# Routing of two neighbouring 1024-token units in one set of instructions, in an agent-attention and top-1 mixture-of-experts kernel

## The chip, the cores and the metric

The kernel runs on one core of a Trainium2 chip. The metric is the device time of one launch in microseconds (us), taken as the median of several executions. A lower time is better.

## The reference

Four batches of 11456 tokens with 128 channels go through an attention with 49 agents, and then every token goes through one of eight experts.

```python
def sm(a, b):                                  # softmax of scaled products
    s = scale * (a @ b.transpose(0, 2, 1))
    e = np.exp(s - s.max(-1, keepdims=True))
    return e / (e.sum(-1, keepdims=True) + 1e-09)
agent_v = sm(agents, k) @ v                    # (4, 49, 128)
x = (sm(q, agents) @ agent_v).reshape(-1, 128) # 45824 tokens

logits = x @ w_gate                            # 8 experts
e_idx = np.argmax(logits, axis=1)
probs = softmax(logits)
gate_w = probs[np.arange(N), e_idx]
eom = 1.0 / (1.0 + np.exp(-(x @ w_output_gate)))
for e in range(E):
    mask = e_idx == e
    h = np.maximum(x[mask] @ w1[e], 0.0)       # 128 -> 1024
    out[mask] = gate_w[mask, None] * eom[mask, e, None] * (h @ w2[e])
```

## The kernel before

**Tiling.** A batch is cut into twelve units (`UNITS`, line 21): eleven of 1024 tokens (128 partitions by 8 tokens) and a last one of 192 tokens (96 partitions by 2). For each batch the kernel makes the agents' averages from k and v, then guesses the expert that most tokens of the batch will take (`fold`, line 666), and runs all tokens of the batch through that one expert in a dense main stream (`mm1` and `mm2`, lines 1009 and 1041, two tiles of 512 tokens for each unit). Tokens that choose another expert are counted, and are computed again afterwards in 14 small "leftover" tiles (`left_prepare`, `left_static`, from line 1377), fetched by indirect DMAs and written over the first result.

**The main stream.** For each tile, TensorE makes hidden values `h` into PSUM banks 0 to 3; ScalarE writes their half-precision upper part `hh` (a relu), VectorE the remainder `hl` (line 1037); then TensorE multiplies both with the second weight into `y`. ScalarE and VectorE add the two halves of `y` into `os` (`finish`, line 1061), GpSimd multiplies `os` by the factor `smt` of each token, and SyncE stores it (`store`, line 1078). `store` begins only when the factor of the unit is in the dictionary `SM`.

**The q side of a unit** (`q_rest`, line 845) has these steps. TensorE has put the scores `qs` into a bank. VectorE takes the maximum `qm` and the difference `qz` (lines 853 to 855), and the bank is free. ScalarE takes the exponential `ef`; ScalarE and GpSimd make a half-precision pair `e16`; SyncE issues a transposing DMA into `x1` and four copies into `x2`. TensorE multiplies `x1` by the gates into `lg` (line 887). ScalarE copies one half of that (`lL`), VectorE adds the other half and makes `d256`. Here `rests[me]` becomes 2. What follows, lines 903 to 933, is called the routing here: 14 VectorE instructions (`rr` twice, `ll`, `lm`, `ld_`, `lr`, `rm`, `oh`, `og`, `ogs`, `se`, `a_` twice, `lT`) and two ScalarE exponentials (`lex`, `eo`), each over the 8 tokens of a partition; then GpSimd makes `smt`, puts the factor beside `ef` and writes the tokens that leave the guessed expert into the table `oht` (lines 936 to 941). SyncE stores `ef` to DRAM (`efd`), and `rests[me]` becomes 3.

**What sets the order.** No instruction order is written by hand. Each part is a Python generator that yields what it would issue next; a planner (`Clock`, line 50) holds an estimated time for each engine and tile from fixed costs (`Engine.cost`, line 153) and lets a generator go on when its inputs should be ready. The result is one fixed instruction list for each engine, which the chip runs in order. `small_products` (line 990) walks through the k, q and v units in a fixed list; `roomy` (line 838) keeps a q unit at most some four units ahead of the main stream, and asks that the logits of the unit five before it are there (`rests` over 1). `q_rest` itself begins only when the unit three before it is wholly done:

```python
while me > 2 and rests[me - 3] < 3 or me > 1 and not state.get(0, {}).get("w"):
    yield None
```

While it waits there it holds the bank of its scores, and `wait_free(True)` allows two such banks at a time. Banks 4 to 7 serve everything but `h`.

In the third batch's end `left_index` (line 1218) begins to put gathers of the leftover tiles into the stream, with VectorE instructions (on tile `big`, shown as `bigs`) that wait for what they bring.

Of the kernel before, what the change touches and what calls it, by code (L numbers as in the profile page):

```python
# [7 lines left out]
F32 = mybir.dt.float32  # L8
# [4 lines left out]
ALU = mybir.AluOpType  # L13
# [3 lines left out]
P = 128  # L17
B, N, C, A, E, F = 4, 11456, 128, 49, 8, 1024
A2 = 50
NB = F // P  # L20
UNITS = [(u * 1024, 128, 8) for u in range(11)] + [(11264, 96, 2)]
# [7 lines left out]
PHASES = [(0, 3, 13, 384), (3, 1, 1, 128)]  # L29
# [213 lines left out]
def agent_attention_top1_moe(ctx, tc, qT, kT, v, aT, wg, wo, w1, w2, cst, out):  # L243
    nc = tc.nc
    clk = Clock()
    ACT, DVE, POOL = Engine(clk, "ACT", nc.scalar), Engine(clk, "DVE", nc.vector), Engine(clk, "POOL", nc.gpsimd)
    PE, SY = Engine(clk, "PE", nc.tensor), Engine(clk, "SP", nc.sync)

    def pool(name, bufs):
        return Tiles(clk, ctx.enter_context(tc.tile_pool(name=name, bufs=bufs)), bufs)  # L250
# [3 lines left out]
    wk = pool("wk", 2)  # L254
# [34 lines left out]
    def release(k):  # L289
        banks[k][0] = True  # L290
# [34 lines left out]
    rank8 = kc[:, K_RANK:K_RANK + E]  # L325
# [17 lines left out]
    for i in range(4):  # L343
        t = cp.tile([P, 8, P], F16, name=f"e16_{i}")
        e16s.append(t)
    avd = []
    for i in range(2):
        t = cp.tile([P, 2, P], F32, name=f"avd_{i}")
# [3 lines left out]
    for i in range(2):  # L352
        t = cp.tile([P, 2, 18], F16, name=f"gs_{i}")
# [3 lines left out]
    for i in range(2):  # L357
        t = cp.tile([P, E, NCOL], F32, name=f"oht_{i}")
# [9 lines left out]
    efd = [dr.tile([n * N, A2], F32, name=f"efd{b0}") for b0, n, _, _ in PHASES]  # L368
# [49 lines left out]
    state = {}  # L418
    picking = [True]
    X1 = {}  # L420
    SM = {}
# [56 lines left out]
    def vacant_turned():  # L478

        return first_place(LARGE, LARGE + SMALL) or first_place(0, LARGE, KEEP)  # L480

    def place(item, k, shape, dt=F32):
        kind, b, u = item
        t = ld.tile([P] + shape, dt, name=f"{kind}{b}_{u}_ld", tag=f"ld{k}", bufs=1)
        places[k] = [False, t.name]
        held[item] = k
        return t
# [51 lines left out]
    NU = len(UNITS)  # L539
# [295 lines left out]

    rests = []

    def roomy(me, n):

        if me < n:  # L840
            return True
        b, u = tiles[max(mains[0] - 1, 0)][0:2]
        return NU * b + u > me - n and rests[me - n] > 1

    def q_rest(b, u, s, mark):
        base, pp, nt = UNITS[u]
        me = len(rests)
        rests.append(0)
        while me > 2 and rests[me - 3] < 3 or me > 1 and not state.get(0, {}).get("w"):
            yield None  # L850
        sv = s[0:pp, 0:nt * A2].rearrange("p (t a) -> p t a", a=A2)[:, :, 0:A]
        m = wk.tile([P, 8], F32, name=f"qm{b}_{u}", tag="qm", bufs=3)
        yield from DVE.q.tensor_reduce(m[0:pp, 0:nt], sv, axis=AX.X, op=ALU.max)
        z = wk.tile([P, 8, A2], F32, name=f"qz{b}_{u}", tag="qz", bufs=3)
        yield from DVE.q.tensor_tensor(z[0:pp, 0:nt, 0:A], sv,
                          m[0:pp, 0:nt].unsqueeze(2).broadcast_to([pp, nt, A]), op=ALU.subtract)
        release(mark)
        ef = wk.tile([P, 8, A2], F32, name=f"ef{b}_{u}", tag="ef", bufs=5)
        ev = ef[0:pp, 0:nt, 0:A]
        yield from ACT.q.activation(ev, z[0:pp, 0:nt, 0:A], AF.Exp, scale=SCALE)  # L860
        e16 = e16s[(NU * b + u) % 4]
        yield from ACT.q.copy(e16[0:pp, 0:nt, 0:A], ev)
        yield from LOW.q.tensor_tensor(e16[0:pp, 0:nt, A:2 * A], ev, e16[0:pp, 0:nt, 0:A], op=ALU.subtract)
        yield from POOL.q.tensor_copy(e16[0:pp, 0:nt, 2 * A:P], ev[:, :, 0:AD])
        while me > 0 and rests[me - 1] < 1:
            yield None
        while vacant_turned() is None:
            yield None
        x1 = place(("x1", b, u), vacant_turned()[1], [1024], F16)
        yield from SY.q.dma_start(x1[:, 0:nt * pp].rearrange("p (t c) -> p t c", c=pp), e16[0:pp, 0:nt, :],  # L870
                                  transpose=True)
        while vacant_turned() is None:
            yield None
        x2 = place(("x2", b, u), vacant_turned()[1], [1024], F16)
        for g in range(G4):
            yield from SY.q.dma_start(x2[32 * g:32 * g + AR, 0:nt * pp], x1[AD:A, 0:nt * pp])
        X1[b, u] = x1, x2
        rests[me] = 1
        while not {"gs", "ndom"} <= state.get(b, {}).keys() or (me > 0 and rests[me - 1] < 2):
            yield None  # L880
        gs, s3, ndom = state[b]["gs"], state[b]["s3"], state[b]["ndom"]
        ohb = oht[b % 2]
        yield from wait_free()
        lg = bank(f"lg{b}_{u}")
        mark = hold()
        for t in range(nt):
            yield from PE.q.matmul(lg[0:pp, t * 36:(t + 1) * 36], x1[:, t * pp:(t + 1) * pp],
                                   gs.rearrange("p k c -> p (k c)"), start=True, stop=True)

        def tl(nm, *sh):  # L890
            return wk.tile([P, 8, *sh], F32, name=f"{nm}{b}_{u}", tag=nm, bufs=3)[0:pp, 0:nt]

        lv = lg[0:pp, 0:nt * 36].rearrange("p (t a) -> p t a", a=36)
        L = tl("lL", 16)
        yield from ACT.q.copy(L, lv[:, :, 18:34])
        d256 = tl("d256")
        yield from DVE.q.tensor_scalar(d256, lv[:, :, 16], 1e-9, None, op0=ALU.add)
        yield from DVE.q.tensor_tensor(L, lv[:, :, 0:16], L, op=ALU.add)
        release(mark)
        rests[me] = 2  # L900
        while not clk.started:
            yield None
        rr = tl("rr")
        yield from DVE.q.tensor_scalar(rr, d256, s3[0:pp], None, op0=ALU.mult)
        yield from DVE.q.reciprocal(rr, rr)
        l = tl("ll", 16)
        yield from DVE.q.tensor_tensor(l, L, rr.unsqueeze(2).broadcast_to([pp, nt, 16]), op=ALU.mult)
        lm = tl("lm")
        yield from DVE.q.tensor_reduce(lm, l[:, :, 0:E], axis=AX.X, op=ALU.max)
        d = tl("ld_", E)  # L910
        yield from DVE.q.tensor_tensor(d, l[:, :, 0:E], lm.unsqueeze(2).broadcast_to([pp, nt, E]), op=ALU.subtract)
        r = tl("lr", E)
        yield from DVE.q.scalar_tensor_tensor(r, d, 0.0, rank8[0:pp].unsqueeze(1).broadcast_to([pp, nt, E]),
                                 op0=ALU.is_ge, op1=ALU.mult)
        rm = tl("rm")
        yield from DVE.q.tensor_reduce(rm, r, axis=AX.X, op=ALU.max)
        oh = tl("oh", E)
        yield from DVE.q.tensor_tensor(oh, r, rm.unsqueeze(2).broadcast_to([pp, nt, E]), op=ALU.is_equal)
        og = tl("og", E)
        yield from DVE.q.tensor_tensor(og, oh, l[:, :, E:2 * E], op=ALU.mult)  # L920
        ogs = tl("ogs")
        yield from DVE.q.tensor_reduce(ogs, og, axis=AX.X, op=ALU.add)
        ex = tl("lex", E)
        yield from ACT.q.activation(ex, d, AF.Exp)
        eo = tl("eo")
        yield from ACT.q.activation(eo, ogs, AF.Exp, scale=-1.0)
        se = tl("se")
        yield from DVE.q.tensor_reduce(se, ex, axis=AX.X, op=ALU.add)
        a_ = tl("a_")
        yield from DVE.q.scalar_tensor_tensor(a_, se, 1e-9, d256, op0=ALU.add, op1=ALU.mult)  # L930
        yield from DVE.q.scalar_tensor_tensor(a_, eo, 1.0, a_, op0=ALU.add, op1=ALU.mult)
        T = tl("lT")
        yield from DVE.q.reciprocal(T, a_)
        while "i12" not in state[b]:
            yield None
        smt = wk.tile([P, 8], F32, name=f"smt{b}_{u}", tag="smt", bufs=12)
        yield from POOL.q.tensor_scalar(smt[0:pp, 0:nt], T, state[b]["i12"][0:pp], None, op0=ALU.mult)
        SM[b, u] = smt
        yield from POOL.q.tensor_copy(ef[0:pp, 0:nt, A], T)
        yield from POOL.q.tensor_tensor(ohb[0:pp, :, 8 * u:8 * u + nt].rearrange("p e t -> p t e"), oh,  # L940
                           ndom[0:pp].unsqueeze(1).broadcast_to([pp, nt, E]), op=ALU.mult)
        ph = phase(b)
        r0 = (b - PHASES[ph][0]) * N + base
        yield from SY.q.dma_start(efd[ph][r0:r0 + pp * nt, :].rearrange("(p t) a -> p t a", t=nt), ef[0:pp, 0:nt, :])
        rests[me] = 3
        if u == NU - 1:
            yield from q_tail(b)

    def phase(b):
        return max(i for i, x in enumerate(PHASES) if x[0] <= b)  # L950
# [506 lines left out]
    with tc.For_i(0, some, 1):  # L1457
        for ph, (b0, nb, nst, rows) in enumerate(PHASES):
            nr = nc.values_load(nti[ph][0:1, 0:1], min_val=0, max_val=rows,
                                skip_runtime_bounds_check_because="at most one tile per 128 tokens and one per group")  # L1460
            with tc.For_i(nst, nr, 1) as i:
                ti, tu, ef, oa = drain(left_index(ph, i, 1, f"d{ph}"))
# [59 lines left out]
```

## Time and profile before

| | us |
|---|---|
| median of 3 runs | 1071.93 (1071.73 to 1074.43) |
| the profiled execution's own time | 1073.62 |
| its span, first to last instruction | 1071.6 |
| VectorE: `hl<-h,hh` 128x512, 704 instructions, busy | 437.7 |
| ScalarE busy | 592.6 |
| GpSimd busy | 275.2 |
| mean granted TensorE clock over the span | 0.984 of full speed |

A page of the profile gives for each engine the time in which it was busy, groups of like instructions with their count, busy time and mean duration, and the idle time ahead of them with what ended it. PE is TensorE, DVE is VectorE, ACT is ScalarE, POOL is GpSimd, SP is SyncE. Since one helper issues everything, nearly all instructions bear line 193, and a group is known by its tiles: `ll<-lL,rr` is the instruction that writes `ll` from `lL` and `rr`. Matmul ends are modelled, so that a busy PE need not be at its peak; its waits and the distance between its starts say more.

### The profile page before, as it was taken

The page shows a single profiled execution, that of the slowest core. Times are in us where ns is not written, and L with a number is a line of the kernel's source. Part 1 is how long each engine was busy: PE and PEld are TensorE (multiplying, and loading weights), DVE is VectorE, ACT ScalarE, POOL GpSimd, SP SyncE. Part 2 cuts the span into 40 slices and gives each one's busy share as a digit, 9 for nine tenths or more (in the row PEclk, how much of TensorE's full clock was granted, in tenths as well). Part 3 has the DMA queues.
Part 4 walks back from the last instruction along what each step waited for, and adds up shares of the span by engine and source line. Part 5 has one row for each costly group of instructions (what it writes and reads, how often), then busy time and mean ns, then how long its engine had stood idle before and what let it go on. Part 6 is the DMA issues. An engine that isn't in the chain of part 4 may idle for free. (4 is left out here: it accounts for less than half of the span.)

```text
span 1071.6 us, 27654 instructions
## 1 busy us (share of the span) xinstructions
PE 1033.2 (96%) x10671; PEld 840.9 (78%) x10671; DVE 859.9 (80%) x2344; ACT 592.6 (55%) x1396; POOL 275.2 (26%) x440
## 2 busy tenths in 40 slices
PE   9989899999999999999999999999899999999996
PEld 9977777788788877778788788777677676788885
DVE  2738699888988898888988888989989978877551
ACT  2325456565755665556755665556645554655552
POOL 0301123222121232232121232321123263521121
PEclk9999899999999999999999999999999998999998
DMA  8785854444557444453466544446232732644430
GB/s 293 231 213 156 193 117 146 125 122 136 133 141 197 141 134 112 119 147 116 111 185 166 153 125 119 129 123 171 73 75 56 168 92 78 149 136 130 131 124 28
DMA packets 108818, 147.13 MB, mean 137 GB/s; under 512 B 61128, under 2 KB 71548, under 8 KB 108682
## 3 DMA queue, kind: packets, MB, share of 16 engines
q1 hardware_dynamic: 107338, 143.83, 48.4%
q0 software_dynamic: 1344, 1.49, 0.8%
q8 instruction: 85, 1.39, 0.5%
q14 instruction: 51, 0.42, 0.1%
HBM read 91.86 MB, written 35.17 MB: 119 GB/s over the span
## 5 line engine op out<-in xcount | busy, mean ns | idle before, releaser
L193 PE MATMUL y<-vv,hh 128*128 128x256 f16 (+1 forms) x2880 | 593.0, 275 | 4.3 <-DVE w L193 3.1
L193 PE MATMUL y<-vv,hl 128*128 128x128 f16 (+1 forms) x2880 | 532.7, 220 | 3.3 <-DVE hl L193 2.5
L193 DVE SCALAR_TENSOR_TENSOR hl<-h,hh 128x512 f16<-128x512 f32 (+1 forms) x736 | 447.0, 667 | 85.3 <-ACT hh L193 84.2
L193 ACT ACTIVATE hh<-h 128x512 f16<-128x512 f32 (+1 forms) x736 | 372.2, 591 | 231.3 <-PE h L193 231.0
L193 PEld LDWEIGHTS <-hh 128*128 128x128 f16 (+1 forms) x2880 | 284.7, 99 | 67.0 <-issue 37.1
L193 PEld LDWEIGHTS <-hl 128*128 128x128 f16 (+1 forms) x2880 | 320.7, 112 | 10.9 <-DVE hl L193 6.2
L193 PE MATMUL h<-x_ld,w 128*128 128x512 f16 (+1 forms) x1472 | 289.4, 379 | 12.1 <-DVE hl L193 11.5
L193 PEld LDWEIGHTS <-w 128*128 128x128 f16 x1472 | 98.3, 103 | 105.0 <-issue 84.7
L193 POOL TENSOR_TENSOR os<-os,smt 128x512 f32<-128x512 f32 (+1 forms) x92 | 94.3, 1025 | 234.8 <-issue 168.9
L193 ACT COPY ys<-y 128x256 f32<-128x256 f32 x180 | 67.4, 374 | 99.6 <-PE y L193 97.4
L193 PEld LDWEIGHTS qs<-at,q_ld 128*128 128x128 f32 x720 | 112.0, 190 | 7.0 <-DVE km_m L193 0.3
L193 PE MATMUL qs<-at,q_ld 128*128 128x50 f32 x720 | 114.0, 245 | 0.0
L193 PE MATMUL ks<-at,k_ld 128*128 128x50 f32 x720 | 111.4, 257 | 2.2 <-DMA k_ld<-kT 2.2
L193 PEld LDWEIGHTS ks<-at,k_ld 128*128 128x128 f32 x720 | 109.2, 195 | 5.5 <-DMA k_ld<-kT 3.1
L193 PE MATMUL av<-ev,v_ld 128*128 128x50 f32 x720 | 110.7, 251 | 0.0
L193 PEld LDWEIGHTS av<-ev,v_ld 128*128 128x128 f32 x720 | 107.6, 191 | 1.8 <-ACT ev L193 0.2
L193 DVE TENSOR_TENSOR os<-y,ys 128x256 f32<-128x256 f32 x180 | 75.0, 417 | 30.3 <-ACT ys L193 22.4
L193 POOL TENSOR_TENSOR e<-ef,e 128x392 f16<-128x392 f32 (+1 forms) x48 | 41.8, 870 | 151.9 <-ACT e L193 93.4
L193 POOL TENSOR_TENSOR ev<-S,km_o 128x400 f32<-128x400 f32 (+1 forms) x44 | 41.1, 935 | 150.7 <-PE av L193 108.6
L193 POOL TENSOR_SCALAR smt<-lT,i 128x8 f32<-128x8 f32 (+1 forms) x48 | 14.8, 309 | 130.6 <-DVE lT L193 109.9
L193 PEld LDWEIGHTS <-idle_x 128*128 128x128 f16 x305 | 45.9, 158 | 2.7 <-DVE idle_x L193 1.1
L193 PE MATMUL lh<-lxs,lw 128*128 128x128 f32 x224 | 42.9, 276 | 0.0
(200 smaller groups left out, 1041.3 us busy)
## 6 DMA issues: line engine op xcount, KB each, us to landing
q_ld<-qT SPq DMA_DIRECT2D x44, 512.0 KB
v_ld<-v SPq DMA_DIRECT2D x44, 512.0 KB
out<-os SPq DMA_DIRECT2D x88, 256.0 KB
k_ld<-kT SPq DMA_DIRECT2D x43, 512.0 KB
lw<-w SPq DMA_DIRECT2D x28, 512.0 KB
efd<-ef SPq DMA_DIRECT2D x44, 200.0 KB
x_ld<-x_ld SPq DMA_DIRECT2D x176, 38.0 KB
w1t<-w SPq DMA_DIRECT2D x8, 256.0 KB
```

Source lines behind the costliest of these rows:

```text
L193: return getattr(self.eng, op)(*a, **k)
```

## The change

Units 0 to 9 of a batch go in pairs; units 10 and 11 go alone. The first unit of a pair runs as far as its logits, writes them into the first half of tiles that are twice as wide, and ends there. The second unit writes the other half, and then issues each routing instruction once over both units (16 tokens in a partition). The tiles have two buffers in place of three, and `smt` has 6 buffers of 16 columns in place of 12 of 8. The two copies into `ef`, and the two stores of `ef`, stay one for each unit. Both units' `rests` become 3 after the store that belongs to each, at the end of the pair.

```diff
+    R = {}
...
+        pair, n2 = u < NU - 2, 2 * nt if u < NU - 2 else nt
+        o = nt * (u % 2) if pair else 0
+        if o == 0:
+            R[b, u] = {}
+
         def tl(nm, *sh):
-            return wk.tile([P, 8, *sh], F32, name=f"{nm}{b}_{u}", tag=nm, bufs=3)[0:pp, 0:nt]
+            t = R[b, u - 1 if o else u]
+            if nm not in t:
+                t[nm] = wk.tile([P, 16, *sh], F32, name=f"{nm}{b}_{u}", tag=nm, bufs=2)
+            return t[nm][0:pp, 0:n2]
...
-        yield from ACT.q.copy(L, lv[:, :, 18:34])
+        Lu = L[:, o:o + nt]
+        yield from ACT.q.copy(Lu, lv[:, :, 18:34])
         d256 = tl("d256")
-        yield from DVE.q.tensor_scalar(d256, lv[:, :, 16], 1e-9, None, op0=ALU.add)
-        yield from DVE.q.tensor_tensor(L, lv[:, :, 0:16], L, op=ALU.add)
+        yield from DVE.q.tensor_scalar(d256[:, o:o + nt], lv[:, :, 16], 1e-9, None, op0=ALU.add)
+        yield from DVE.q.tensor_tensor(Lu, lv[:, :, 0:16], Lu, op=ALU.add)
         release(mark)
         rests[me] = 2
+        R[b, u - 1 if o else u].setdefault("efs", []).append((u, me, ef))
+        if pair and o == 0:
+
+            return
         while not clk.started:
             yield None
         rr = tl("rr")
+        bc = lambda x, n: x.unsqueeze(2).broadcast_to([pp, n2, n])
...
-        yield from DVE.q.tensor_tensor(l, L, rr.unsqueeze(2).broadcast_to([pp, nt, 16]), op=ALU.mult)
+        yield from DVE.q.tensor_tensor(l, L, bc(rr, 16), op=ALU.mult)
...
-        smt = wk.tile([P, 8], F32, name=f"smt{b}_{u}", tag="smt", bufs=12)
-        yield from POOL.q.tensor_scalar(smt[0:pp, 0:nt], T, state[b]["i12"][0:pp], None, op0=ALU.mult)
-        SM[b, u] = smt
-        yield from POOL.q.tensor_copy(ef[0:pp, 0:nt, A], T)
-        yield from POOL.q.tensor_tensor(ohb[0:pp, :, 8 * u:8 * u + nt].rearrange("p e t -> p t e"), oh,
-                           ndom[0:pp].unsqueeze(1).broadcast_to([pp, nt, E]), op=ALU.mult)
+        smt = wk.tile([P, 16], F32, name=f"smt{b}_{u}", tag="smt", bufs=6)
+        yield from POOL.q.tensor_scalar(smt[0:pp, 0:n2], T, state[b]["i12"][0:pp], None, op0=ALU.mult)
+        ef_s = R.pop((b, u - 1 if o else u))["efs"]
+        c0 = 8 * ef_s[0][0]
+        for k, (uu, mm, x) in enumerate(ef_s):
+            SM[b, uu] = smt[:, k * nt:(k + 1) * nt]
+        for k, (uu, mm, x) in enumerate(ef_s):
+            yield from POOL.q.tensor_copy(x[0:pp, 0:nt, A], T[:, k * nt:(k + 1) * nt])
+        yield from POOL.q.tensor_tensor(ohb[0:pp, :, c0:c0 + n2].rearrange("p e t -> p t e"), oh,
+                           ndom[0:pp].unsqueeze(1).broadcast_to([pp, n2, E]), op=ALU.mult)
         ph = phase(b)
-        r0 = (b - PHASES[ph][0]) * N + base
-        yield from SY.q.dma_start(efd[ph][r0:r0 + pp * nt, :].rearrange("(p t) a -> p t a", t=nt), ef[0:pp, 0:nt, :])
-        rests[me] = 3
+        for uu, mm, x in ef_s:
+            r0 = (b - PHASES[ph][0]) * N + UNITS[uu][0]
+            yield from SY.q.dma_start(efd[ph][r0:r0 + pp * nt, :].rearrange("(p t) a -> p t a", t=nt), x[0:pp, 0:nt, :])
+            rests[mm] = 3
```

More of the change, by code (lines that the diff above doesn't have):

```diff
@@ L910, in q_rest @@
         d = tl("ld_", E)
-        yield from DVE.q.tensor_tensor(d, l[:, :, 0:E], lm.unsqueeze(2).broadcast_to([pp, nt, E]), op=ALU.subtract)
+        yield from DVE.q.tensor_tensor(d, l[:, :, 0:E], bc(lm, E), op=ALU.subtract)
         r = tl("lr", E)
-        yield from DVE.q.scalar_tensor_tensor(r, d, 0.0, rank8[0:pp].unsqueeze(1).broadcast_to([pp, nt, E]),
+        yield from DVE.q.scalar_tensor_tensor(r, d, 0.0, rank8[0:pp].unsqueeze(1).broadcast_to([pp, n2, E]),
                                  op0=ALU.is_ge, op1=ALU.mult)
@@ L917, in q_rest @@
         oh = tl("oh", E)
-        yield from DVE.q.tensor_tensor(oh, r, rm.unsqueeze(2).broadcast_to([pp, nt, E]), op=ALU.is_equal)
+        yield from DVE.q.tensor_tensor(oh, r, bc(rm, E), op=ALU.is_equal)
         og = tl("og", E)
```

## The prediction

> **What bounds the kernel now.** I read the page first, for the engines' shares and for how they lie over the span. These are its span, its busy times, and the slices of VectorE.
>
> ```profile
> span 1071.6 us, 27654 instructions
> PE 1033.2 (96%) x10671; PEld 840.9 (78%) x10671; DVE 859.9 (80%) x2344; ACT 592.6 (55%) x1396; POOL 275.2 (26%) x440
> ...
> DVE  2738699888988898888988888989989978877551
> ```
>
> TensorE has work nearly all the time. VectorE, from which the change takes work, is at 80% over the whole, and at eight or nine tenths through the middle. A busy matmul row is modelled, so the second view is the list of what TensorE waited for. Its columns are the total in us, the number of waits, and the longest.
>
> ```profile
> PE h L193 <- DVE hl L193: 11.5, 33, 3.6
> PE lg L193 <- DMA x_ld<-e: 3.7, 1, 3.7
> PE y L193 <- DVE w L193: 3.1, 1, 3.1
> PE y L193 <- DVE hl L193: 2.5, 3, 1.5
> ```
>
> The three VectorE rows come to 17.1 us. That is the most that a faster VectorE can give back directly, out of 1071.6. The third view, busy time in four stages, says where. After the bounds and the length come PE, PEld, DVE, ACT and POOL, the granted clock, the DMA share and GB/s.
>
> ```profile
> 0.00:150.00 150.00, 141.07 (x1423) 124.99 (x1424) 95.71 (x278) 60.76 (x142) 27.94 (x54) 0.95 0.76 208
> 150.00:740.00 590.00, 583.24 (x6239) 472.25 (x6237) 518.66 (x1391) 354.31 (x828) 149.22 (x251) 1.00 0.49 136
> 740.00:900.00 160.00, 148.09 (x1432) 110.40 (x1429) 140.77 (x391) 87.12 (x207) 49.09 (x70) 0.96 0.39 96
> 900.00:1072.00 172.00, 160.79 (x1587) 133.25 (x1583) 104.77 (x287) 90.42 (x219) 48.96 (x65) 0.98 0.39 118
> ```
>
> From 150 to 740 us, where k, v and q products are mixed into the main stream, TensorE is idle for 590 - 583.24 = 6.8 us at full clock: this stage is bound by TensorE. From 740 to 900 us it is idle for 11.9 us, and its clock of 0.96 takes 0.04 x 160 = 6.4 us more. VectorE is 88% busy there (140.77 of 160). The remainder of its time in this stage is mostly no slack, as its own waits show:
>
> ```profile
> DVE bigs L193 <- DMA bigs<-cumd,lrus: 6.2, 1, 6.2
> DVE bigs L193 <- DMA out<-os: 3.4, 1, 3.4
> ```
>
> For 9.6 us VectorE stands at instructions of the leftover tiles that wait for a DMA, and everything queued behind them stands too. 140.8 + 9.6 is 150.4 of 160 us, so VectorE all but sets the pace there. TensorE's waits of this stage say the same:
>
> ```profile
> PE h L193 <- DVE hl L193: 6.0, 8, 3.6
> PE y L193 <- DVE w L193: 3.1, 1, 3.1
> PE y L193 <- DVE hl L193: 2.3, 2, 1.5
> ```
>
> Those of the stage from 150 to 740 us are many and short:
>
> ```profile
> PE h L193 <- DVE hl L193: 5.1, 23, 0.2
> ```
>
> **The change part by part.** First, what a unit's routing costs on VectorE now (busy us, mean ns of one, idle time before), and two shapes of one instruction, from which the price of an element comes:
>
> ```profile
> L193 DVE TENSOR_SCALAR rr<-d,s_s 128x8 f32<-128x8 f32 x44 | 14.5, 332 | 0.0
> L193 DVE RECIPROCAL rr<-rr 128x8 f32<-128x8 f32 x44 | 8.5, 194 | 0.1
> L193 DVE TENSOR_TENSOR ll<-lL,rr 128x128 f32<-128x128 f32 x44 | 14.1, 320 | 0.4
> L193 DVE TENSOR_REDUCE lm<-ll 128x8 f32<-128x64 f32 x44 | 9.3, 211 | 0.4
> L193 DVE TENSOR_TENSOR ld<-ll,lm 128x64 f32<-128x64 f32 x44 | 14.6, 332 | 0.3
> L193 DVE SCALAR_TENSOR_TENSOR lr<-ld,kc 128x64 f32<-128x64 f32 x44 | 15.2, 344 | 0.5
> L193 DVE TENSOR_REDUCE rm<-lr 128x8 f32<-128x64 f32 x44 | 9.5, 216 | 0.5
> L193 DVE TENSOR_TENSOR oh<-lr,rm 128x64 f32<-128x64 f32 x44 | 14.6, 332 | 0.7
> L193 DVE TENSOR_TENSOR og<-oh,ll 128x64 f32<-128x64 f32 x44 | 14.0, 318 | 0.9
> L193 DVE TENSOR_REDUCE ogs<-og 128x8 f32<-128x64 f32 x44 | 9.5, 215 | 0.6
> L193 DVE TENSOR_REDUCE se<-lex 128x8 f32<-128x64 f32 x44 | 9.1, 206 | 0.0
> L193 DVE SCALAR_TENSOR_TENSOR a<-se,d 128x8 f32<-128x8 f32 x44 | 10.6, 240 | 0.4
> L193 DVE SCALAR_TENSOR_TENSOR a<-eo,a 128x8 f32<-128x8 f32 x44 | 10.5, 239 | 1.7
> L193 DVE RECIPROCAL lT<-a 128x8 f32<-128x8 f32 x44 | 8.9, 202 | 1.2
> ...
> L193 DVE SCALAR_TENSOR_TENSOR hl<-h,hh 128x512 f16<-128x512 f32 x704 | 437.7, 682 | 81.8 <-ACT hh L193 80.8
> ...
> L193 DVE SCALAR_TENSOR_TENSOR hl<-h,hh 128x192 f16<-128x192 f32 x32 | 9.3, 350 | 3.5 <-ACT hh L193 3.4
> ```
>
> The 14 means add up to 3.70 us for a unit. An element costs (682 - 350) / (512 - 192) = 1.04 ns. A pair's instruction carries a second unit's elements: 128 more for `ll`, 64 more for each of eight instructions, 8 more for each of five, 680 in all, or 0.71 us. So a pair costs 4.41 us where two units cost 7.40, and saves 2.99 us. With 5 pairs in each of 4 batches that is 20 x 2.99 = 60 us of summed durations and 280 fewer instructions. Busy time falls by less, since windows of neighbouring instructions overlap: 704 `hl` of 682 ns are 480 us, and their row says 437.7, some 60 ns each; 280 x 60 ns is 17 us. I expect DVE busy at 800 to 817 us, from 859.9.
>
> [...]
>
> On ScalarE 40 exponentials go, and on GpSimd 40 instructions of `smt` and `oht`. I cost both at nothing: ACT is 55% busy and POOL 26%, and this saving would show only where one of them was late. The copies into `ef` and SyncE's stores stay as many. The two stores now stand in SyncE's queue one behind the other, at the time of the second; no later instruction of the pair is between them. TensorE's instructions are the same ones.
>
> What is moved: the first unit's factors come with the second's. `roomy` lets the scores of unit 9 begin only when the main stream is at unit 5, and these two rows of batch 1 are unit 7's `smt` and unit 9's `qm`:
>
> ```profile
> 425.38 0.30 POOL L193 TENSOR_SCALAR smt<-lT,i 128x8 f32<-128x8 f32 x1 [3.28 <-DVE lT L193]
> ...
> 433.35 0.56 DVE L193 TENSOR_REDUCE qm<-qs 128x8 f32<-128x392 f32 x1
> ```
>
> So pair 6 and 7 would be done while the main stream is still in unit 5, before any tile of unit 6 needs its `SM`. Its cover is one whole unit of the main stream. The wait that the change adds is at the head of `q_rest`: unit 9 needs `rests` of unit 6 at 3, which is now the end of the pair. Queued behind it is unit 9's own chain, and it holds a bank. With 433.35 - 425.38 = 8 us to spare it costs nothing here; the pair's chain grows by 0.7 us.
>
> Now the sum, in the profiled execution, whose own time is 1073.62 us, 2.0 over its span and 1.7 over the median of 1071.93. In the stage from 740 to 900 us alone, the first and the last routing group have these counts:
>
> ```profile
> L193 DVE TENSOR_TENSOR ll<-lL,rr 128x128 f32<-128x128 f32 x8 | 2.9, 359 | 0.1
> ...
> L193 DVE RECIPROCAL lT<-a 128x8 f32<-128x8 f32 x7 | 1.4, 199 | 0.1
> ```
>
> Seven to eight units are three and a half pairs, 3.5 x 2.99 = 10.5 us off a VectorE that sets the pace for part of the stage. Bounds: nothing, if only the DMA waits and `w` count, which routing does not touch; 18.3 us, if all idle time and the whole clock loss go (11.9 + 6.4). I take 4.0, under half of 10.5, because the largest single waits (3.6 and 3.1 us) stand behind other things. From 150 to 740 us the bounds are 0 and 5.1 us; a unit pair now puts 14 instructions ahead of `hl` where it put 28, so I take a third less waiting, rounded down to 1.4. Ahead of 150 us (a DMA wait) and after 900 us I count nothing. Together -5.4: a span of 1066.2, an own time of 1068.2, and a median of 1066.5 us.
>
> **The rivals.** *Nothing to be seen.* TensorE sets the end, the short waits are bank handovers that any order has, and the last batch's losses are its two DMA waits. For it: 583.24 of 590 us. The gain is then the 1.4 and little else, and the time is 1069 to 1074.
>
> *A new stall at the start; slower.* In batch 0 the pipeline has no lead yet. These are unit 3's `smt`, and the `qm` of units 5 and 6:
>
> ```profile
> 137.91 0.34 POOL L193 TENSOR_SCALAR smt<-lT,i 128x8 f32<-128x8 f32 x1 [0.36 <-DVE ld L193]
> ...
> 118.68 0.56 DVE L193 TENSOR_REDUCE qm<-qs 128x8 f32<-128x392 f32 x1
> ...
> 140.72 0.55 DVE L193 TENSOR_REDUCE qm<-qs 128x8 f32<-128x392 f32 x1
> ```
>
> Unit 5 must now wait for pair 2 and 3, so its `qm` goes from 118.68 to about 138, next to unit 6's. Two sets of transposes are then issued within some 3 us, and `lg` stands in TensorE's fixed order at a place set by the estimated landing. One such miss is in the trace: `lg` waited 3.7 us for `x1`. The clock in that stage was 0.95, which is 7.5 us lost; if half of it belongs to this stall, a second one costs 3.7 + 3.7 = 7.4 us. Against it: DMA share falls after 150 us (0.76 to 0.49). It decides once the new wait exceeds what is gained; with the 1.4 kept, the time is 1071.9 + 7.4 - 1.4 = 1077.9, or 1075 to 1078 for a shorter wait.
>
> *VectorE is the bound throughout.* Then all 43 to 60 us of its saving come off: 1012 to 1029. Against it stand the 17.1 us of TensorE's waits on it. [...]
>
> That the pairs do not come about is excluded: the list is fixed, and forms of 128x16 will be there or not.
>
> **How the numbers follow.** Forecast 0.48, with its own range of 1057 to 1069; nothing to be seen 0.28; new stall 0.20; VectorE as the bound 0.04. About 0.3%, or 3.2 us, is what a measurement here can tell from no change. Faster by more: 0.45 of the forecast, 0.02 of "nothing", 0.04 of the last, 0.51. Within: 0.03, 0.24 and 0.03 of the stall, 0.30. Slower: 0.02 and 0.17, 0.19. The range goes from 1056, a little under the forecast's own end, since 1071.9 - 18.3 = 1053.6 is the case of a stage wholly healed, to 1078 for the stall.
>
> **What would show it.** Right: 20 instructions of each routing group with twice the elements, `ll` near 0.45 us; DVE at 800 to 817 us with 280 fewer; TensorE's idle time of 740 to 900 us down by some 4 us with its clock, and the stage before it hardly changed. Wrong: the wait `h <- DVE hl` as long as before although DVE is less busy, which is the first rival; a wait of `lg` for `x_ld` at 140 to 165 us, which is the second; or the two waits of `bigs` for a DMA grown, which the planner's new order can do and which I count in no term.

## The result, and the profile after

The kernel with pairs is slower. Its median is 1086.09 us (1085.75 to 1086.55, 4 runs), against 1073.18 us for the kernel before on the same chip; the ratio is 1.0121, with a 95% interval of 1.0102 to 1.0139. The forecast was 1066.5 us, in a range of 1056 to 1078: the sign and the range both missed. The profiled execution took 1086.55 us, with a span of 1084.6, so that 13.0 us of span came on top. Two of the experiments below, the one with pairs in the first three batches and the one with pairs in the last, had one execution each at a lower clock, some 5% longer; their ratios are of the others.

The page of the kernel after has these lines for span, busy time and VectorE's forty slices:

```profile
span 1084.6 us, 27290 instructions
PE 1035.6 (95%) x10671; PEld 842.6 (78%) x10671; DVE 831.9 (77%) x2064; ACT 589.2 (54%) x1356; POOL 264.3 (24%) x400
...
DVE  2748688898878788889878888888968766666662
```

VectorE issues 280 instructions fewer (2344 to 2064), as forecast, and is busy for 28.0 us less (859.9 to 831.9). TensorE's busy time has hardly moved (1035.6 us for 1033.2). So less work took longer, and idle time must have grown. The same four stages as before, with the same columns:

```profile
0.00:150.00 150.00, 141.52 (x1441) 125.14 (x1442) 93.64 (x242) 60.08 (x137) 27.36 (x50) 0.98 0.73 207
150.00:740.00 590.00, 582.70 (x6240) 472.55 (x6237) 506.56 (x1225) 352.96 (x808) 143.59 (x226) 1.00 0.50 137
740.00:900.00 160.00, 142.32 (x1335) 106.70 (x1332) 125.21 (x316) 81.03 (x186) 44.25 (x60) 0.93 0.38 92
900.00:1085.00 185.00, 169.01 (x1665) 138.25 (x1661) 106.48 (x284) 95.10 (x228) 49.06 (x66) 0.98 0.40 111
```

From 150 to 740 us VectorE lost 12.1 us of work and TensorE's idle time is 7.3 us where it was 6.8. The loss lies from 740 to 900 us: TensorE is idle for 17.7 us (before: 11.9) and its granted clock of 0.93 costs an estimated 0.07 x 160 = 11.2 us (before: 6.4). That is 5.8 + 4.8 = 10.6 of the 13.0 us. The stages around it nearly cancel: after 900 us TensorE is idle for 4.8 us more (16.0 for 11.2), and up to 150 us a clock of 0.98 in place of 0.95 gives back an estimated 4.5. Of the estimated 4.8 us of clock, 2.0 lie ahead of 780 us, where the clock was 0.91 (before: 0.96); idle time there is the same in both.

A count of the main stream's `hl` instructions shows the same without any modelled time. These are VectorE's `hl` alone, up to 780 us and from there to 900, first before, then after:

```profile
0.00:780.00 780.00, 328.22 (x536) 0.99 0.54 149
780.00:900.00 120.00, 54.33 (x92) 0.96 0.38 91
```

```profile
0.00:780.00 780.00, 329.36 (x538) 0.99 0.54 149
780.00:900.00 120.00, 49.11 (x85) 0.93 0.38 89
```

At 780 us the kernel after is two instructions ahead. At 900 us it is five behind (623 to 628). The stretch in between is the last batch, with the leftover tiles in the stream. What TensorE waited for from 740 to 900 us of the kernel after, the five largest rows:

```profile
PE y L193 <- DVE hl L193: 4.7, 2, 4.5
PE h L193 <- DVE hl L193: 3.9, 6, 2.7
PE y L193 <- DVE w L193: 3.1, 1, 3.1
PE ly L193 <- ACT lh L193: 2.6, 1, 2.6
PE lg L193 <- ACT let_sb L193: 2.1, 1, 2.1
```

Against the rows of before in the prediction, the waits for `hl` have hardly grown in sum (8.6 us for 8.3), and the wait for `w` is the same 3.1. What is new are the two rows of ScalarE, 4.7 of the 5.8 us. VectorE's own waits at the leftover tiles, from 740 to 900 us, are

```profile
DVE bigs L193 <- DMA bigs<-ppid: 4.8, 1, 4.8
DVE bigs L193 <- DMA out<-os: 2.4, 1, 2.4
DVE bigs L193 <- DMA bigs<-cumd,lrus: 1.5, 1, 1.5
```

or 8.7 us, where the kernel before had 9.6 (6.2 and 3.4). They stand in other places and are not longer in sum.

The longest wait of TensorE, 4.5 us, can be followed back in three time lines. TensorE of the kernel after first (start, duration, then the idle time before it and what ended it), then its VectorE, then its SyncE:

```profile
804.92 0.29 PE L193 MATMUL y<-vv,hl 128*128 128x128 f16 x1 [4.50 <-DVE hl L193]
805.00 0.42 PE L193 MATMUL y<-vv,hh 128*128 128x256 f16 x1
```

```profile
797.23 0.55 DVE L193 TENSOR_REDUCE qm<-qs 128x8 f32<-128x392 f32 x1
802.57 0.42 DVE L193 TENSOR_TENSOR bigs<-bigs,lrs 128x256 f32<-128x256 f32 x1 [4.80 <-DMA bigs<-ppid]
...
804.18 2.48 DVE L193 SCALAR_TENSOR_TENSOR hl<-h,hh 128x512 f16<-128x512 f32 x4
```

```profile
798.47 1.21 SPq L193 DMA_DIRECT2D bigs<-ppid  x2
```

SyncE issues the load of `ppid` at 798.47 us. VectorE reached the step of the leftover tiles that compares with it at 797.8 us and stands there until 802.57. Four `hl` of the main stream are queued behind it, and the `y` matmuls wait for them. Then the clock is down, at 0.83 from 800 to 810 us: the 128x256 matmul behind the stall took 0.42 us, where its group's mean is 0.275. In the kernel before, the first of the two loads of `ppid` was issued 5.4 us earlier (the second at 795.05 us), and the step stood for less:

```profile
793.06 0.37 SPq L193 DMA_DIRECT2D bigs<-ppid  x1
```

```profile
798.02 0.43 DVE L193 TENSOR_TENSOR bigs<-bigs,lrs 128x256 f32<-128x256 f32 x1 [3.41 <-DMA out<-os]
```

A second stall at a step that compares with `ppid` follows in the kernel after, on VectorE and then on TensorE:

```profile
843.27 1.63 DVE L193 TENSOR_TENSOR bigs<-bigs,lrs 128x1408 f32<-128x1408 f32 x1 [2.39 <-DMA out<-os]
```

```profile
845.55 2.92 PE L193 MATMUL h<-x_ld,w 128*128 128x512 f16 x8 [2.67 <-DVE hl L193]
```

The tiles `let_sb` and `lh` in TensorE's list of waits are leftover tiles too. So the trace puts the growth of idle time on the leftover tiles' steps, on ScalarE's more than on VectorE's, and none of it on routing. That it stands there does not say why: the pairs might push the chain of the last batch out of step (the new wait), or the planner might simply have laid the instructions in a less lucky order.

### The profile page after: what moved, and what is told of

It reads as the page before. It is cut to its first block, busy times and chain, and to the rows that moved or that the text cites. A ratio compares the mean times of both kernels' runs of the same rounds, so it can differ in the third digit from the quotient of the medians.

```text
span 1084.6 us, 27290 instructions
## 1 busy us (share of the span) xinstructions
PE 1035.6 (95%) x10671; PEld 842.6 (78%) x10671; DVE 831.9 (77%) x2064; ACT 589.2 (54%) x1356; POOL 264.3 (24%) x400
## 5 line engine op out<-in xcount | busy, mean ns | idle before, releaser
L193 PE MATMUL ly<-lw,lh 128*128 128x128 f32 x224 | 44.1, 281 | 2.6 <-ACT lh L193 2.6
L193 ACT COPY S<-ks 128x400 f32<-128x400 f32 (+1 forms) x48 | 23.0, 481 | 38.3 <-PE ks L193 38.1
```

Source lines behind the costliest of these rows:

```text
L193: return getattr(self.eng, op)(*a, **k)
```

## The experiments

Three theories stood against each other. **A**: the wait that the change adds (the second unit of a pair cannot begin its `q_rest` until the pair before it is wholly done) holds the scores of odd units and throws the last batch out of step. In the profile after, the `qm` of two units lie 0.56 us apart at 839.76 and 840.32 us, so that odd units were held. **B**: the pairs cost nothing themselves; a different list of costs gives the planner a different order, and the order decides in the last batch. **D** says where B acts: at the places where VectorE stands in order at a step of the leftover tiles. The expectations also name **C** (the wide instructions cost, or the factors come late), **E** (pairs in the last batch come late and two units at a time, whatever the leftover tiles do) and **S** (the pairs lose some us apart from the order). Each ratio below is to the kernel before on the same chip, whose median was 1070.5 to 1071.6 us.

**The wait loosened.** On the kernel after, the second unit of a pair waits for less:

```diff
-        while me > 2 and rests[me - 3] < 3 or me > 1 and not state.get(0, {}).get("w"):
+        odd = u < NU - 2 and u % 2
+        while (me > 2 and rests[me - 3] < (2 if odd else 3) or odd and me > 4 and rests[me - 5] < 3
+               or me > 1 and not state.get(0, {}).get("w")):
```

> Changed kernel, but the second unit of a pair no longer waits at the head of q_rest for the end of the pair before it: it may begin once the unit three before it has its logits and the unit five before it is done. Theory A (the new wait at the head of q_rest: in the last batch it holds back the scores of units 5, 7 and 9 by 20, 35 and 16 us, so that two units' chains come at once into the stage of the leftover tiles): the loss of some 17 us after unit 2 of the last batch goes, 1068 to 1074 us. Theory B (no part of the change is to blame, any new order meets the leftover tiles' DMA waits in another way): anything from 1068 to 1090. Theory C (the wide instructions, or factors that come late): 1084 to 1088.

Measured: 1079.13 us, 1.0081 (1.0054 to 1.0108). A third of the loss is back, less than A needs and more than C allows. The trace shows the old picture with other lengths; these are VectorE's waits for DMAs from 740 to 960 us:

```profile
DVE bigs L193 <- DMA efd<-ef: 5.6, 1, 5.6
DVE bigs L193 <- DMA bigs<-ppid: 5.1, 1, 5.1
DVE bigs L193 <- DMA bigs<-cumd,lrus: 3.3, 1, 3.3
```

They come to 14.0 us, more than the 8.7 of the kernel after, which is 7 us slower. So the sum of these stalls alone does not rank the kernels.

**The wait alone.** On the kernel before, with nothing paired, the counters that other units wait on rise as they do with pairs:

```diff
-        rests[me] = 3
+        if u >= NU - 2:
+            rests[me] = 3
+        elif u % 2:
+            rests[me - 1] = rests[me] = 3
```

> Kernel before, with routing unit by unit as it was, but an even unit counts as done only when the odd one after it is: the new wait at the head of q_rest alone. Theory A: slower than before by 8 to 15 us, 1081 to 1088. Theory B: 1073 with a spread of a few us either way. Theory C: as before, 1071 to 1075.

Measured: 1071.24 us, 0.9998 (0.9978 to 1.0018). The wait by itself costs nothing in the order that it was laid in here. With this, A loses its ground.

**Pairs in the first three batches only, and in the last only.**

```diff
-        pair, n2 = u < NU - 2, 2 * nt if u < NU - 2 else nt
+        pair = u < NU - 2 and b < B - 1
+        n2 = 2 * nt if pair else nt
```

The other kernel has `b == B - 1`. In both, a single unit keeps its place in the order by a wait for the unit two before it, and `smt` has 12 buffers.

> Changed kernel with pairs in batches 0 to 2 and single units in the last batch (smt with 12 buffers, and a single unit's routing tiles wait for the unit two before it). Theory A and C: the 2 to 4 us that the changed kernel was ahead up to the last batch stay and the loss goes, 1067 to 1072. Theory B: anything from 1067 to 1085.

> Changed kernel with single units in batches 0 to 2 and pairs in the last batch alone. Theory A and C: the loss without the early gain, 1086 to 1092. Theory B: anything from 1068 to 1090.

Measured: 1071.82 us, 1.0009 (0.9992 to 1.0026), with 15 pairs in batches 0 to 2; 1076.44 us, 1.0065 (1.0041 to 1.0089), with 5 pairs in the last batch. In this order, fifteen of twenty pairs are worth nothing that can be measured, although VectorE's waits at `bigs` came to 11.2 us there. Five pairs in the last batch go with half of the loss; whether the pairs or the new order bring it, this run does not tell.

**The leftover tiles' steps later.** In `left_index`, ahead of the comparison with `ppid` and of the one with `cumd`, the planner is told to hold the step back for 8 us. The rest of the list goes on in the meantime:

```diff
         rb = r.unsqueeze(2).broadcast_to([P, n, P])
+        yield from pause(8000.0 if n > 1 else 0.0)
         yield from DVE.q.tensor_tensor(c, pb, rb, op=ALU.is_le)
...
+        yield from pause(8000.0 if n > 1 else 0.0)
         yield from DVE.q.tensor_tensor(cr, cr, ppx.unsqueeze(2).broadcast_to([P, n, NCOL]), op=ALU.is_le)
```

> Changed kernel, with the leftover tiles' two VectorE steps that wait for a DMA (the comparison after the ppid loads, the comparison after the cumd gathers) let into VectorE's list 8 us of estimated time later. Theory D (the loss is VectorE standing at those steps, since with pairs in the last batch SyncE issues the ppid loads some 5 us later than the estimate has it; everything queued behind stands, TensorE idles and loses clock): most of the loss goes, 1070 to 1077. Theory E (pairs in the last batch come late and two units at a time, whatever the leftover tiles do): 1082 to 1088. Theory B (any new order gives another time): anything from 1066 to 1088.

> Kernel before, with the same two steps let in 8 us of estimated time later. Theory D: its own two such waits (3.4 and 6.2 us) and the clock behind them go, 1060 to 1067. Theory E: as before or a little faster, 1066 to 1072. Theory B: 1064 to 1080.

Measured: with pairs 1071.51 us, 1.0004 (0.9988 to 1.002); without pairs 1073.03 us, 1.0004 (0.9987 to 1.0021). With pairs the whole loss is gone, against E, and the list of VectorE's waits has no DMA wait of `bigs` from 740 to 960 us. Without pairs there is no gain, against what D expected. Why is seen at the end of the main stream. This is its last group of `y` matmuls from 1036 us on (the times behind the three durations are the first and the last start), of the kernel before, of the kernel before with the pause, and of the kernel after with the pause:

```profile
L193 PE MATMUL y<-vv,hl x72: 219/219/230, 1035.9 to 1059.1; 128*128 128x128 f16 x56, 128*96 128x128 f16 x16
```

```profile
L193 PE MATMUL y<-vv,hl x46: 219/219/229, 1035.8 to 1050.2; 128*128 128x128 f16 x30, 128*96 128x128 f16 x16
```

```profile
L193 PE MATMUL y<-vv,hl x32: 219/219/230, 1035.9 to 1044.1; 128*128 128x128 f16 x16, 128*96 128x128 f16 x16
```

The main stream ends 9 us earlier without pairs, and with pairs 28 us earlier than the 1072.2 us of the kernel after. But the spans are 1071.9 and 1071.2 us: what comes last now is the tail of the leftover tiles, 22 and 27 us of it, where it is some 12 us in both kernels. With the pause of 8 us the main stream ended earlier, and the tail took the gain.

**Half the pause.** The same edits with 4000 in place of 8000.

> Changed kernel, the leftover tiles' two waiting steps let in 4 us later in place of 8. In the run with 8 us the main stream ended 28 us sooner than in the changed kernel, but the leftover tiles came late and 27 us of tail stood after it. Theory D (VectorE standing at those steps is the loss): the main stream still ends some 10 to 20 us sooner than in the changed kernel, the tail is shorter, 1062 to 1070. Theory B (the order decides): 1066 to 1082.

> Kernel before with the same two steps 4 us later. Theory D: its waits of 3.4 and 6.2 us mostly go without the long tail, 1062 to 1068. Theory B: 1066 to 1080.

Measured: with pairs 1066.19 us, 0.9954 (0.9938 to 0.9969); without pairs 1058.52 us (1057.18 to 1061.14), 0.9893 (0.9876 to 0.9911). The second has no pair in it and beats both kernels, the one before by 1.1% and, taking the two ratios together (0.9893 / 1.0121), the one after by some 2.3%; it is also faster than the 1062 us at which D's range began. Its stage from 740 to 920 us, in the columns of the four stages, and VectorE's only wait for a DMA there:

```profile
740.00:920.00 180.00, 172.39 (x1726) 131.40 (x1724) 162.00 (x457) 105.26 (x251) 67.55 (x95) 0.98 0.37 101
```

```profile
DVE bigs L193 <- DMA bigs<-cumd,lrus: 0.7, 1, 0.7
```

The same stage of the kernel before and of the kernel after:

```profile
740.00:920.00 180.00, 168.09 (x1643) 126.01 (x1641) 156.20 (x432) 99.68 (x238) 64.89 (x90) 0.96 0.41 97
```

```profile
740.00:920.00 180.00, 160.00 (x1507) 119.39 (x1504) 136.09 (x335) 92.01 (x211) 58.20 (x75) 0.93 0.40 91
```

Of the two without pairs, the faster one has the busier VectorE (162.00 us for 156.20) and gets more matmuls done on TensorE (1726 for 1643). So VectorE's load does not set the pace of this stage. The fastest of the three has 0.7 us of stalls at `bigs` left; the other two, with 9.6 and 8.7 us, are not ranked by them. With pairs, the half pause leaves two waits for `ppid`, 5.6 us together and the longer of them 4.2 us; TensorE has a wait for `hl` of 4.3 us in the same stage.

**Another order, nothing else.** `Engine.cost` gives the planner a fixed cost of 68 ns for a VectorE instruction. It enters no instruction; it only shifts the estimates by which the order is laid.

```diff
-            return 68.0 + n * per + (65.0 if len(ins) > 2 or op == "tensor_scalar" and len(ins) > 1 else 0.0)
+            return 70.0 + n * per + (65.0 if len(ins) > 2 or op == "tensor_scalar" and len(ins) > 1 else 0.0)
```

The same was done with 66 and with 72, each on the kernel before and on the kernel after.

> Kernel before with one number of the planner's cost table changed (fixed part of a VectorE instruction 70 in place of 68 ns): the same instructions in a slightly other order. It measures how much the order alone moves the time. Theory B: over 4 us from the kernel before, either way. Theories D and E: within 3 us of it.

> Changed kernel with the same number changed. Theory B: over 4 us from the changed kernel's 1086, most likely towards 1075. Theories D and E: within 3 us of 1086.

> Kernel before with 66 in place of 68 in the planner's cost table: one more order of the same instructions. Theory B: anything from 1066 to 1082. A systematic loss by pairs (theory S, some 5 us apart from the order) needs the orders of before to lie at 1070 to 1076 on the mean.

> Changed kernel with 66 in place of 68. Theory B: anything from 1066 to 1086, no different on the mean from orders of the kernel before. Theory S: 1076 to 1086.

> Kernel before with 72 in the planner's cost table. Orders of this kernel so far: 1071, 1080, 1080. Theory B: 1066 to 1082.

> Changed kernel with 72. Orders of it so far: 1086, 1078, 1077. Theory B: 1066 to 1086, within 8 us of the run before it, on either side. Theory S: slower than the run before it by 3 us or more.

Measured, in us, with the ratio to the kernel before as it is and its interval:

| fixed cost | without pairs | with pairs |
|---|---|---|
| 66 ns | 1079.59; 1.0093 (1.0076 to 1.011) | 1076.76; 1.0064 (1.0047 to 1.0081) |
| 68 ns (as it is) | 1 | 1086.09; 1.0121 (1.0102 to 1.0139) |
| 70 ns | 1079.84; 1.0078 (1.0051 to 1.0104) | 1077.52; 1.0065 (1.0033 to 1.0096) |
| 72 ns | 1087.9; 1.0144 (1.0113 to 1.0175) | 1077.06; 1.0047 (1.0024 to 1.0069) |

Two nanoseconds in a table move the kernel without pairs by 8 to 9 us, and four by 16, more than the change under study. In three of the four rows the pairs are the faster ones (by 3, 2 and 11 us), where at 66 and 70 the intervals overlap; only at 68 are they slower (by 13). The kernel before happened to stand at the best of its four orders, the kernel after at the worst of its four. The means of the two columns are alike, 1.0079 and 1.0074, which speaks against S; four orders that lie up to 16 us apart cannot tell a gain of 5 us from none.

Here D, which in the expectations allowed 3 us for another order, falls as the whole account, and 72 ns without pairs lies even outside B's 1066 to 1082 us. Nor does all of the swing lie at the leftover tiles. At 66 ns without pairs VectorE stands at a `bigs` step for a DMA for 5.4 us from 740 to 960 us, but some of the loss is older than that. This is the count of `hl` up to 740 us, and TensorE's wait of `h` for `hl` from 150 to 740 us (total in us, number of waits; the longest is 0.2 or 0.3):

| fixed cost | `hl` without, with pairs | wait without pairs | wait with pairs |
|---|---|---|---|
| 66 ns | 508, 512 | 7.3, 33 | 4.2, 18 |
| 68 ns (as it is) | 511, 512 | 5.1, 23 | 4.9, 23 |
| 70 ns | 504, 508 | 6.0, 27 | 4.2, 19 |
| 72 ns | 502, 512 | 7.9, 36 | 4.5, 21 |

Without pairs the three other orders are 3 to 9 instructions behind before any leftover tile is reached, and in these three the pairs take 1.8 to 3.4 us off the wait.

By the same measure every run above is one order too. A difference of some 8 us or less cannot be credited to its edit. The half pauses stand outside: 1058.52 us without pairs is 12 us under the best of the four orders without pairs, and 1066.19 with pairs some 10 us under the best of the four with pairs.

**Without the leftover tiles.** The pairs must show their own worth once the leftover tiles are gone from the stream; the tokens that choose another expert then keep the main stream's result. On both kernels:

```diff
             yield from left_table(ph)
+            continue
...
-    spawn(left_static(), 5)
-    spawn(left_scatter(), 3)
```

> Kernel before without the static leftover tiles: their tables are still made, but none is gathered, computed or stored, so those tokens keep the main stream's result. It is the base for the next run. Some 31 us of TensorE work and the DMA waits of the last batch are gone: 1010 to 1035 us.

> Changed kernel without the static leftover tiles. Theory B (TensorE sets the pace everywhere else, so that 43 to 60 us less VectorE work and the new wait are both worth nothing, and the loss was the order of the leftover steps): within 3 us of the base. Theory S (pairs come late in the last batch, two units at a time): 5 us or more slower than the base. The prediction's own theory (less VectorE work, less waiting of TensorE): 3 us or more faster.

Measured: without pairs 1004.26 us, 0.9378 (0.935 to 0.9406); with pairs 1005.64 us, 0.9387 (0.9359 to 0.9415). The base came out under the 1010 to 1035 us expected, which counted 31 us of TensorE's work: its busy time fell by 63.8 us (1033.18 to 969.40). The stage from 740 to 900 us, without pairs and with them:

```profile
740.00:900.00 160.00, 154.74 (x1591) 116.50 (x1589) 149.43 (x395) 95.69 (x227) 34.99 (x63) 0.99 0.30 78
```

```profile
740.00:900.00 160.00, 154.56 (x1587) 117.14 (x1587) 133.05 (x322) 95.42 (x218) 32.64 (x52) 0.98 0.31 78
```

With pairs VectorE is busy for 16.4 us less in this stage alone, at 93% busy without them, and TensorE does the same work in the same time. Neither a price nor a saving is seen: the difference of 1.4 us lies within the intervals. That goes against C, E and S as well. TensorE's waits for `hl` over the whole span, without pairs and with them, say why:

```profile
PE h L193 <- DVE hl L193: 7.7, 35, 0.2
PE y L193 <- DVE hl L193: 2.4, 4, 1.0
```

```profile
PE h L193 <- DVE hl L193: 6.0, 28, 0.2
PE y L193 <- DVE hl L193: 3.2, 5, 1.1
```

No wait of `h` is over 0.2 us, a short handover. The pairs bring 1.7 us less of it and 0.8 us more of the other row, which is below what the measurement can tell. Where VectorE's time went is seen at its `hl` from 740 to 900 us, without pairs and with them:

```profile
L193 DVE SCALAR_TENSOR_TENSOR hl<-h,hh 128x512 f16<-128x512 f32 x128 | 79.4, 680 | 6.0 <-ACT hh L193 5.6
```

```profile
L193 DVE SCALAR_TENSOR_TENSOR hl<-h,hh 128x512 f16<-128x512 f32 x128 | 79.4, 681 | 16.8 <-ACT hh L193 16.8
```

The same 128 instructions now wait 11 us longer for ScalarE's `hh`.

## Why the prediction was wrong

**The work removed: right in its price, too large in busy time.** The pair's 14 instructions were forecast at 4.41 us. Groups of the kernel after (busy us, mean ns of one, idle time before):

```profile
L193 DVE TENSOR_TENSOR ld<-ll,lm 128x128 f32<-128x128 f32 x20 | 11.5, 573 | 0.1
...
L193 DVE TENSOR_TENSOR ll<-lL,rr 128x256 f32<-128x256 f32 x20 | 9.2, 460 | 0.1
...
L193 DVE TENSOR_TENSOR oh<-lr,rm 128x128 f32<-128x128 f32 x20 | 5.8, 290 | 0.3
...
L193 DVE RECIPROCAL lT<-a 128x16 f32<-128x16 f32 x20 | 5.0, 251 | 0.6
```

All 14 means add up to 4.38 us, and `ll` took 460 ns where 0.45 us was forecast. The busy time was to fall to 800 to 817 us and fell to 831.9. The durations being as forecast (4.38 us for 4.41), the term for overlapping windows was too small: it was 60 ns for each instruction removed, or 17 us of 60, and what showed was 60 - 28 = 32 us.

**The step that failed: "I take 4.0, under half of 10.5", from 740 to 900 us.** It rested on the sum of 140.8 us busy and 9.6 us of waits for DMAs, from which "VectorE all but sets the pace there" was read. The two halves of that sum are different things. The busy half was no bound: with the leftover tiles gone, 16.4 us less of it gave nothing. The waiting half was kept as it was, as something "which routing does not touch"; the new list laid it anew, in three places of 8.7 us in place of two of 9.6, and put 4.7 us of waits for ScalarE's leftover steps and an estimated 4.8 us of clock beside it. Where the sum counted -4.0, the stage came to +10.6, and no experiment shows the pairs themselves to have a share in it. The prediction named a part of this under what would show it wrong, the "two waits of `bigs` for a DMA grown, which the planner's new order can do and which I count in no term". One of the two grew (3.4 to 4.8 us) and the other shrank (6.2 to 1.5), so that the sign itself did not come as named. The mistake behind it holds: the order of a planned list had been treated as free, and its swing of up to 16 us is three times the whole forecast gain of 5.4. That the order makes the difference is shown by the shifted cost; by which of its stalls it does so in the kernel after is read from the trace alone.

**From 150 to 740 us: -1.4 forecast, nothing found.** TensorE's wait of `h` for `hl` in this stage is

```profile
PE h L193 <- DVE hl L193: 4.9, 23, 0.2
```

against 5.1 us before, with the same 23 waits. Here the rival "nothing to be seen" was right, which called them handovers that any order has. But their number is not fixed: at 66, 70 and 72 ns it fell with the pairs, by 1.8 to 3.4 us, so that a saving of the forecast kind shows in this row in three orders of four, though each of them compares two different lists.

**The new wait at the head of `q_rest`: rightly costed at nothing**, by the experiment with the wait alone. The 8 us to spare were read from batch 1; in the last batch odd units were held, and what loosening the wait gave back (7 us) is no more than another order can give.

**The rivals.** "A new stall at the start" had the sign and the wrong place: TensorE is idle for 8.5 us up to 150 us where it was 8.9, at a clock of 0.98. "Nothing to be seen" was the true one for the pairs by themselves, as far as one order each can tell (15 pairs: 1.0009; without leftover tiles: 1004.26 and 1005.64), with a chance of 0.28; its time of 1069 to 1074 us missed as well, since it too took the order as given. "VectorE is the bound throughout" is excluded by the same two runs.

**What stays open.** ScalarE stood 4.99 us at a leftover step (`lh`, at 885.93 us of the kernel after) for something that the profile calls remote, which no run took apart; TensorE's new waits for ScalarE hang on it in part. The SyncE queue lies in another order in the two kernels, but which earlier instruction held its load of `ppid` back was not followed. With pairs and half a pause the main stream ends 21 us earlier (1051.4 for 1072.2) although a wait of 4.2 us stays, which the removed stalls alone do not make up. The orders were tried at four values of one cost; how wide the whole spread is, they do not tell, nor why without pairs three of them fall behind before 740 us.

## What to carry to other kernels

Where a planner lays the order, shift one of its costs by a few per cent and time that first: here it moved the same work by up to 1.4%, and a change that promises less cannot be judged on one order. Work taken off an engine can be worth nothing: without the leftover tiles, 16.4 us less of VectorE from 740 to 900 us gained no time that could be measured, where TensorE's single waits for `hl` were 1.0 us at the longest. So look at the length of single waits (0.2 us is a handover here) and not at the busy share, nor at busy time plus waits. Compare lists of waits row by row, before and after: a long stall that is new may stand for another that is gone (VectorE's at `bigs` came to 8.7 us in three places where there had been 9.6 in two). An engine that stands in order at a load can be helped by moving that step later, as far as the tail at the end allows: without pairs 4 us gained 1.1%, and 8 us nothing.

## What the runs showed of the hardware

Behind some of TensorE's waits the granted clock was down, and by how much did not follow their length. In the kernel after, the wait of 4.5 us that ended at 804.92 us was followed by 128x256 matmuls of 0.42 us, and the granted clock from 800 to 810 us was 0.83. In the kernel before, TensorE's wait ahead of the same ten microseconds was 1.04 us (it ended at 799.56), and the clock was 0.83 as well. After first, then before:

```profile
800.00:810.00 10.00, 5.50 (x48) 3.43 (x47) 6.21 (x18) 3.40 (x9) 1.84 (x3) 0.83 0.30 75
```

```profile
800.00:810.00 10.00, 9.40 (x83) 6.50 (x83) 8.42 (x24) 4.85 (x13) 2.88 (x3) 0.83 0.20 45
```

By estimate that is 0.17 x 10 = 1.7 us in both. Behind a wait of 1.45 us in the kernel before, which ended at 815.03 us, the clock stayed at 1.00 (810 to 830 us). The wait for `w`, 3.1 us in both kernels, had a clock of 0.83 behind it before and of 0.66 after (750 to 760 us). So the lengths of the waits do not tell a stage's clock loss here. That a wait brings the clock down is read from the order in time; no run varied it.

Instructions of one size and one kind did not cost the same: `ld` of 128x128 took 573 ns in the mean, and `oh` of the same shape and operation 290. Ten of the twenty `ld` took 274 to 292 ns, the other ten 437 to 1090. Each of these ten began while GpSimd was in a tensor_tensor of its own, and ended some 0.15 us after that one, as here at 154.63 and 154.49 us:

```profile
153.45 1.04 POOL L193 TENSOR_TENSOR os<-os,smt 128x512 f32<-128x512 f32 x1 [7.20 <-issue]
153.54 1.09 DVE L193 TENSOR_TENSOR ld<-ll,lm 128x128 f32<-128x128 f32 x1
```

Of the ten short ones, only one began during such an instruction, 0.06 us before its end. That VectorE was held by GpSimd is read from these times; no run varied it. The row of `ld` in the prediction, 332 ns, is such a mean too: 35 of its 44 took 173 to 253 ns, and eight of the other nine ran into a GpSimd tensor_tensor in the same way. Two of the 35 began 0.01 and 0.02 us after the start of such an instruction (`e<-ef,e`) and were short all the same, 0.20 and 0.22 us.

A reciprocal paid more by the element than a reduction: 8 elements more took `lT` from 202 to 251 ns, 6.1 ns each, where 64 more took `rm` from 216 to 282, 1.0 ns each.
